# A forward and backward of a recurrent-memory transformer block on one core: merged dP products, a planner with later landings, and Wo turned in runs

## The chip, the cores and the metric

The kernel runs on one core of a Trainium2 chip. The metric is the time of one execution in microseconds on the device, the median of several runs; lower is better.

## The reference

For x of 2048 tokens by 512, xn = layernorm(x), and the output is x + A(xn) + B(xn).

B is a dense layer pair: h = relu(xn w1 + b1) squared, then h w2 + b2, with w1 of 512 by 1792.

A is an attention with a recurrent memory. The 2048 tokens are cut into 64 segments of 32. For each segment in order, the 8 memory rows are put ahead of its 32 tokens, and 32 heads of width 128 attend over these 40 rows:

```
h = concatenate([mem, xs]);  q, k, v = h Wq, h Wk, h Wv
p = softmax(where(mask, q k^T * scale, -1e9));  o = p v;  o = o Wo
mem = o[:, :M];  outs.append(o[:, M:])
```

The mask lets the memory rows see everything and the tokens see what lies before them. Segment s+1 needs the memory of segment s, so the 64 segments are a chain. The task also asks for the gradients of all ten differentiable inputs for a given grad_out, so the same chain is walked a second time, from the last segment to the first.

## The kernel before, in words

The kernel works in stages, one after the other, all on one core.

The dense part computes the layernorm, B forward and most of B's backward in eight blocks of 256 tokens. It loads w1, w2 and b1 first (L887 to L895), turns w2 and w1 by TensorE transposes (turn_w, L838), and stores the hidden activations and their gradients to DRAM (S_AT, S_GT1).

The forward recurrence walks 64 steps, 16 blocks of four. A step (chain, L1136) projects q, k and v of its 32 rows for all heads (Stage.proj, L530, 32 products of 512 columns each), copies them out of PSUM, transposes q and k, forms scores, takes the softmax weights into the tile P40, multiplies with v, transposes the result, multiplies with Wo (wo_part, L1030) and brings the 8 new memory rows to the next step. q, k, v, P and o are written to DRAM for the backward. Four heads' products stand side by side in four groups of 32 columns of the array, so that four products run together. What is not on this path is filled in around it: the "leading" tokens (the eight rows of each segment that stand in the memory's places, 32 per block: l_proj, l_attn), the outputs of a block (blk_out, L1214) and the weight gradients of w1 and w2 (dw_unit, L1238: for two column blocks at a time, 16 products each with a 128-row block of tokens that is loaded from DRAM into one of five tiles sx).

At the end of this stage, turn_o (L497) turns Wo in place: eight transposes go into one PSUM bank, and two copies bring them back to SBUF. The heads' inner index is taken up in four strides of the bank, so that each copy reads PSUM with jumps.

The backward recurrence walks the steps from the last to the first. A step (chain, L1454) multiplies the step's gradient rows with the turned Wo (gO), copies it to gN, transposes it (gOT), forms dP with the stored v (L1468, products of 40 columns), goes through the softmax backward on VectorE (smax_bwd, L1350, four operations), forms dv, dk and dq (blocks, mixed, diag), transposes each (sq_T, L513) and multiplies with the turned Wv, Wk, Wq into one PSUM bank (dh_part, L1363, ps_dRA); the 8 rows of that sum are the memory gradient that the next step needs (L1524). A block's leading tokens are handled by l_pre (L1381) and l_post (L1420); l_pre forms their dP (ps_dPL, L1404), once against the leading v (VTL) and once against the memory-place v (VTM, the tile LT1), each with products of 32 columns. l_post reads back their gradients from DRAM into dLN and adds ps_dRL.

The last stage computes the gradients of Wq, Wk, Wv and Wo from what was stored (L1690, L1694) and, beside it, the layernorm backward.

The order of the instructions in the first three stages is drawn up when the kernel is built, by a planner (the class _Plan). Every operation has an engine, a cost in microseconds, keys that it reads and writes, and for DMAs a latency after which its data are taken to have landed. The planner ranks the operations by the longest way to the end plus a bias from a table (BIAS_1, BIAS_2; one number for each operation of a scope), then fills the engines' queues in simulated time. PAR gives three parameters for each stage: a grace for operations of low priority, how long an engine is held idle for something better, and a penalty for changing the shape of TensorE's products. The planner also models how TensorE's instructions arrive: in lines of 128 products, a line no sooner than 4.2 us after the one before. That count starts with each stage. The order within each engine's queue is then fixed, and an engine waits at the head of its queue until the data are there. SyncE (SP) issues most DMAs, GpSimd (POOL) some.

The helpers Stage.put and Stage.dma (L474, L477) give a DMA its cost (0.5 on POOL, T_DMA = 0.42 on SP) and latency (3.5 and 3.2 unless given); dmaT (L1376) gives a transposing load 1.35 and 3.2. evict (L526) is a copy out of PSUM for which the planner chooses VectorE or ScalarE.

Of the kernel before, what the change touches and what calls it, by code (L numbers as in the profile page):

```python
# [12 lines left out]
BIAS_1 = {  # L13
    "l_proj": (
        47.2, 6.5, -41.1, 1.2, 0.8, -33.9, -14.2, 11.4, 20.3, -5.1, -5.3, -14.4, 17.4, 1.5, 7, 20.1, 4.7,
        25.3, -22.2, 55.6, -37, 19.3, -97.5, -1.4, 23, -6.1, -29.3, 48.8, 4.1, 4.5, 52.1, -159.3,
    ),
    "blk_in": (
        11.4, -35.6,
    ),  # L20
# [4 lines left out]
    ),  # L25
    "chain": (
# [4 lines left out]
    ),  # L31
    "blk_out": (
        16.8, -102.8, -36.2, -171.6, -10.2, -72.7, -50.6, -74.7, -96.5, 48.6,
    ),
    "l_attn": (
# [45 lines left out]
P = 128  # L81
# [227 lines left out]
def kernel(  # L309
# [148 lines left out]
    class Stage:  # L458


        def __init__(self, plan, pool, ways):
            self.plan = plan
            self.pool = pool
            self.ways = ways
            self.cnt = {}
# [1277 lines left out]
```

## Time and profile before

| | |
|---|---|
| time, median of 3 runs | 2799.88 us (2797.52 to 2802.31) |
| span of the profiled execution | 2798.3 us |
| TensorE: products, weight loads | 54888 recorded, 55072 |
| TensorE busy | 2664.6 us (95%) |
| VectorE, ScalarE, GpSimd busy | 1327.3, 985.8, 824.8 us |
| DMA | 530.91 MB, 190 GB/s |
| granted TensorE clock | 0.995 |

The span runs from the first to the last instruction of one execution that was profiled; its own time is this span and the little that lies around it, and the median of the timed runs is 1.6 us above the span. In the rows of the profile PE is TensorE's products, PEld its weight loads, DVE is VectorE, ACT ScalarE, POOL GpSimd and SP the engine that issues DMAs; a q behind an engine's name is its sequencer. A group row has the line, the engine, the operation, what it writes and reads, shapes and count, then busy microseconds and the mean in nanoseconds of one, then the idle time before it with what ended that. A row of waits has the waiting instruction, what it waited for, the total in microseconds, how often, and the longest. A row of the timeline has start and length in microseconds. Some records of products are missing in a trace, so weight loads are the better count.

### The profile page before, as it was taken

Reading aid. Unit: us, or ns where it says so; the run is one execution under the profiler, and the core shown is the slowest. Engines: PE = TensorE matmul, PEld = TensorE weight load, DVE = VectorE, ACT = ScalarE, POOL = GpSimd, SP = SyncE. Lnnn points to the kernel's source line nnn. Section 1 sums busy time; section 2 is a strip of 40 time slices with the busy share of each in tenths; the row PEclk is TensorE's granted clock in tenths of the full one; section 3 lists DMA queues with packets and bytes.
Section 4 is the critical chain, followed back from the end, with each engine's and each line's share of the span. In section 5 each row is a group of like instructions: output and inputs, shape, how many; then the busy total and the mean of one; then the engine's idle time right before and its main releaser. Section 6 shows DMA issues by size and latency. Waiting matters only on the chain.

```text
span 2798.3 us, 125071 instructions
## 1 busy us (share of the span) xinstructions
PE 2664.6 (95%) x54888; PEld 1538.5 (55%) x55072; DVE 1327.3 (47%) x3327; ACT 985.8 (35%) x2012; POOL 824.8 (29%) x2431
## 2 busy tenths in 40 slices
PE   8998999999999999999999999999999899999999
PEld 6664555555555555575555555555555444444444
DVE  5544455555455555565455455555455402232322
ACT  4333444444444444364444444444444300000000
POOL 1111111111111111145555555555555301112210
PEclk9999999999999999999999999999999999999999
DMA  6657656555557566647777676777766698788861
GB/s 211 202 172 205 180 160 175 164 166 163 156 169 186 169 185 175 177 118 178 187 181 187 179 189 179 189 192 190 188 182 177 201 344 273 232 255 270 257 185 42
DMA packets 499792, 530.91 MB, mean 190 GB/s; under 512 B 223845, under 2 KB 325398, under 8 KB 497070
## 3 DMA queue, kind: packets, MB, share of 16 engines
q1 hardware_dynamic: 480254, 463.06, 59.9%
q0 software_dynamic: 15056, 53.56, 5.6%
q8 instruction: 430, 7.05, 1.1%
q10 hardware_dynamic: 3936, 6.29, 0.7%
q14 instruction: 116, 0.95, 0.1%
HBM read 249.77 MB, written 237.52 MB: 174 GB/s over the span
## 4 chain that ended last, share of the span: by engine, by line
PE 45%; DVE 4%; issue 3%; DMA 3%; ACT 1%; POOL 1%; SPq 0%; DVEq 0%; ACTq 0%; POOLq 0%
PE ps_gw L1690 14%; PE ps_dRA L1370 8%; PE ps_gw L1694 5%; PE ps_gO L538 3%; PE ps_dRL L1370 3%; PE ps_d L624 2%; DMA dLN<-S_GNL 2%; PE ps_d L573 1%; PE ps_d L599 1%; PE ps_gOT L429 1%; PE ps_d L588 1%; PE ps_gm L1524 1%; PE ps_gL L538 1%; PE ps_dL L1481 1%; PE ps_dP L1468 1%
## 5 line engine op out<-in xcount | busy, mean ns | idle before, releaser
L1370 PE MATMUL ps_dRA<-WA,dT 128*32 128x512 bf16 x6144 | 377.0, 381 | 5.3 <-issue 2.5
L1690 PE MATMUL ps_gw<-WA,WB 128*128 128x512 bf16 x1505 | 330.6, 379 | 1.6
L1690 PEld LDWEIGHTS <-WB 128*128 128x128 bf16 x1896 | 185.4, 98 | 225.0 <-issue 1.7
L538 PEld LDWEIGHTS <-PA 128*32 128x32 bf16 x8192 | 195.4, 96 | 192.3 <-DVE PA L1190 22.3
L435 ACT CAST dN<-ps_d 128x512 bf16<-128x512 f32 x372 | 207.4, 590 | 184.7 <-PE ps_d L599 112.3
L1370 PEld LDWEIGHTS <-dT 128*32 128x32 bf16 x6144 | 151.8, 96 | 154.2 <-DVE dT L517 17.3
L433 DVE CAST gwo<-ps_gw 128x512 bf16<-128x512 f32 x64 | 40.0, 685 | 399.9 <-PE ps_gw L1690 268.5
L435 ACT CAST gwo<-ps_gw 128x512 bf16<-128x512 f32 x64 | 33.1, 598 | 510.2 <-PE ps_gw L1690 357.3
L517 DVE STREAM_TRANSPOSE dT<-dN 128x256 f32<-128x256 f32 x384 | 165.4, 437 | 72.1 <-ACT dN L435 66.5
L1020 POOL TENSOR_TENSOR P<-P,rsA 128x320 bf16<-128x320 bf16 x64 | 46.2, 722 | 458.8 <-DVE rsA L1015 244.1
L624 PEld LDWEIGHTS <-PB 32*32 32x32 bf16 x8192 | 119.8, 92 | 76.4 <-DVE PB L1168 23.9
L1701 POOL DMA_DIRECT2D out_dram<-gwo x96 | 71.6, 753 | 293.9 <-ACT gwo L435 265.1
L538 PE MATMUL ps_q<-WA,PA 128*32 128x512 bf16 x2048 | 145.2, 382 | 5.5 <-DVE PA L1190 3.7
L1039 PE MATMUL ps_RA<-WB,OT 128*32 128x256 bf16 x4096 | 129.0, 277 | 17.7 <-DVE OT L517 13.6
L538 PE MATMUL ps_k<-WA,PA 128*32 128x512 bf16 x2048 | 144.9, 381 | 0.3 <-DVE PA L1190 0.3
L435 ACT CAST kN<-ps_k 128x512 bf16<-128x512 f32 x125 | 73.4, 587 | 194.1 <-PE ps_k L538 172.2
L538 PE MATMUL ps_v<-WA,PA 128*32 128x512 bf16 x2048 | 140.7, 379 | 0.0
L1039 PEld LDWEIGHTS <-OT 128*32 128x32 bf16 x4096 | 103.9, 98 | 46.2 <-DVE OT L517 32.0
L538 PE MATMUL ps_gO<-WB,PA 128*32 128x512 bf16 x2048 | 126.4, 380 | 1.0 <-DVE PA L1528 1.0
L611 POOL COPY BDL<-bPLL 32x64 bf16<-32x64 bf16 x256 | 60.4, 236 | 218.4 <-PE ps_d L573 210.4
L433 DVE CAST qN<-ps_q 128x512 bf16<-128x512 f32 x62 | 42.9, 692 | 171.5 <-PE ps_q L538 169.5
L1254 PE MATMUL ps_dw<-sx,anT 128*128 128x512 bf16 x339 | 108.2, 384 | 6.6 <-DMA sx<-S_XN 2.8
(315 smaller groups left out, 5300.8 us busy)
## 6 DMA issues: line engine op xcount, KB each, us to landing
S_GN<-dN SPq DMA_DIRECT2D x192, 256.0 KB
WA<-S_GN SPq DMA_DIRECT2D x150, 256.0 KB
S_Q<-qN SPq DMA_DIRECT2D x64, 256.0 KB
S_K<-kN SPq DMA_DIRECT2D x64, 256.0 KB
S_V<-vN SPq DMA_DIRECT2D x64, 256.0 KB
S_ON<-oN SPq DMA_DIRECT2D x64, 256.0 KB
bqN<-S_Q SPq DMA_DIRECT2D x64, 256.0 KB
bkN<-S_K SPq DMA_DIRECT2D x64, 256.0 KB
```

What stands on the lines that cost most here:

```text
L433: nc.vector.tensor_copy(out, in_)
L435: nc.scalar.copy(out, in_)
L517: self.plan.add({"DVE": 0.445}, lambda e, half=half: nc.vector.transpose(words(dst, half).rearrange("p (i c r) -> p i c r", i=4, c=2), src ...
L538: nc.tensor.matmul(bk()[32 * j:32 * (j + 1), :], lhsT=win(dc), rhs=Wt(dc, c0), start=(dc == 0), stop=(dc == DC - 1), tile_position=(0, 32 ...
L611: f(q_(dst, j)[:, :, j, 0:c], q_(src_f(), j))
L624: nc.tensor.matmul(bk()[32 * j:32 * j + m, k * P:(k + 1) * P], lhsT=lf(j, i), rhs=rf(j, i), start=(k == 0 and x == 0), stop=(x == n - 1), ...
L1039: nc.tensor.matmul(bk()[32 * c:32 * (c + 1), :], lhsT=sg.rows(OTt, i, j), rhs=Wo[:, JQ * i + j, dh * DH:(dh + 1) * DH], start=(i == 0 and ...
L1254: nc.tensor.matmul(bks[x]()[:], lhsT=anT[x][:, c, :], rhs=sx[z][:], start=(c == 0), stop=(c == TC - 1))
L1370: nc.tensor.matmul(bk()[32 * j:32 * (j + 1), :], lhsT=sg.rows(XT, i, j), rhs=wtf(t, i, j), start=(first and i == 0), stop=(last and i == N ...
L1690: nc.tensor.matmul(bks[n](), lhsT=HNc[:, rc, dc * P:(dc + 1) * P], rhs=gns[y][:, hf * 512:(hf + 1) * 512], start=(y == 0), stop=(y == NRC ...
L1694: nc.tensor.matmul(bks[n](), lhsT=gns[y][:, k * P:(k + 1) * P], rhs=GOc[:, rc, :], start=(y == 0), stop=(y == NRC - 1))
L1701: nc.gpsimd.dma_start(outWs[t][dc * P:(dc + 1) * P, 4 * hf:4 * hf + 4, j, :], wt[:].rearrange("p (i e) -> p i e", i=4))
```

## The change

The change consists of these parts.

- The load of b1 (dense part): 14 rows of 128 numbers, then a TensorE transpose into a PSUM bank and a copy, in place of a load that scatters b1 down the partitions. The loads of w1, w2 and the first gradient block get a planned latency of 2.6 and a cost of 0.85.
- Forward: two tiles P40 that alternate by step; hN is put into the tile PTLL; the token blocks of dw_unit are loaded two at a time into three tiles; the copies into S_VM, S_KM, S_BL, S_HNL and S_GOL are costed at 0.7; the tiles mk and mkl of the masks move into the dense part's pool.
- Planner: PAR and BIAS_1, BIAS_2 are new in all numbers of the two recurrences. Both recurrences are planned with slow = True: DMAs cost 0.47 (SP) and 0.62 (POOL), and latencies below 4.5 are raised by 1.0. In the backward a transposing load costs 1.45 with a latency of 4.2.
- Turn of Wo: the copies read PSUM and write SBUF in runs of 32 numbers. The heads' inner index is thus left in another order, and the copies of gO and gL out of PSUM put it right, reading in steps of 32.
- Five products of the identity with itself are put behind the forward's plan.
- Backward, l_pre: VTL and LT1 become thirds of one tile V3, so that one product of 64 columns takes both. 32 products in place of 64 for each block.

The helper mixed gets three more arguments that no call uses.

```diff
-PAR = ((0.3, 0.3, 0.0), (0.61, 7.94, 4.04), (0.09, 2.05, 17.32))
+PAR = ((0.3, 0.3, 0.0), (0.38, 999.0, 10.03), (0.09, 1.77, 17.22))
...
-        def put(self, out_f, in_f, R, W, prio=1, lat=3.5, cost=0.5):
+        def put(self, out_f, in_f, R, W, prio=1, lat=3.5, cost=None):
+            cost = cost or (0.62 if self.slow else 0.5)
             self.dma(out_f, in_f, R, W, prio, lat, cost, "POOL")
-        def dma(self, out_f, in_f, R, W, prio=1, lat=3.2, cost=T_DMA, eng="SP"):
+        def dma(self, out_f, in_f, R, W, prio=1, lat=3.2, cost=None, eng="SP"):
+            cost = cost or (0.47 if self.slow else T_DMA)
+            if self.slow and lat < 4.5:
+                lat += 1.0
...
-                    self.evict(lambda blk=blk, d=d0 + d: blk[:, :, d * P:(d + 1) * P].rearrange("p j (a c) -> p j a c", c=JQ), bk,
-                               lambda bk=bk, d=d: bk()[:, d].rearrange("p c (j a) -> p j a c", j=JQ), [(okey, g, d)], 1, {"DVE": 0.61, "ACT": 0.59})
+                    self.evict(lambda blk=blk, d=d0 + d: blk[:, :, d * P:(d + 1) * P].rearrange("p j (c a) -> p j c a", c=JQ), bk,
+                               lambda bk=bk, d=d: bk()[:, d].rearrange("p c (j a) -> p j c a", j=JQ), [(okey, g, d)], 1, {"DVE": 0.37, "ACT": 0.59})
...
+                if nm in ("gO", "gL"):
+                    self.evict(lambda half=half: dst[1][:, 4 * half:4 * half + 4, :].rearrange("p i (a c) -> p i a c", c=JQ),
+                               bk, lambda bk=bk: bk()[:].rearrange("p (i c a) -> p i a c", i=4, c=JQ), [(dst[0], half)], prio, EV_F)
+                    continue
...
-                        sg.dma(lambda: b1Tb[:], lambda: B_b1.rearrange("(c p) -> p c", p=P), [], ["b1Tb"], lat=5.0)
+                        sg.dma(lambda: b1Tb[:], lambda: B_b1.rearrange("(c p) -> c p", p=P), [], ["b1Tb"], lat=5.0)
...
-                A({"DVE": 0.1}, lambda e: V.tensor_copy(b1T[:], b1Tb[:]), ["b1Tb"], ["b1T"])
+                bb1 = sg.bank("B", [P, FC], BF16, "ps_b1")
+                A({"PE": 0.1}, lambda e: transpose_to(bb1()[:], b1Tb[:]), ["b1Tb"], [bb1])
+                A({"DVE": 0.1}, lambda e: V.tensor_copy(b1T[:], bb1()[:]), [bb1], ["b1T"])
...
-                z = c % 5
-                sg.dma(lambda z=z: sx[z][:], lambda c=c: src[c * P:(c + 1) * P, :], [], [("sx", z)], lat=3.0)
+                z = c // 2 % 3
+                if c % 2 == 0:
+                    sg.dma(lambda z=z: sx[z][:], lambda c=c: src[c * P:(c + 2) * P, :].rearrange("(c p) d -> p c d", p=P), [], [("sx", z)], lat=3.2)
...
+        with tc.manual_schedule():
+            al = pc.tile([P, 512], F32, name="ps_al", tag="c0")
+            for x in range(5):
+                nc.tensor.matmul(al[:, 0:P], lhsT=ident[:], rhs=ident[:], start=True, stop=True)
...
-        LT0, LT1 = (tl("LT%d" % x, TR) for x in range(2))
+        LT0, V3 = tl("LT0", TR), tl("V3", [P, 3, NI, JQ, RA])
+        VTL, LT1 = [V3[:, 1], V3[:, 0]], V3[:, 2]
+        V2 = [V3[:, 1:3], V3[:, 0:3:2]]
...
-            A({"SP": 1.35}, lambda e: nc.sync.dma_start_transpose(out_f(), in_f()), R, W, prio, 3.2)
+            A({"SP": 1.45}, lambda e: nc.sync.dma_start_transpose(out_f(), in_f()), R, W, prio, 4.2)
...
                 for i in range(NI):
-                    for c, VX in enumerate((VTL[p], VTM)):
-                        for j in range(JQ):
-                            nc.tensor.matmul(q_(bk(), j)[:, i, 32 * c:32 * c + 32], lhsT=LT0[:, i, j, :],
-                                             rhs=VX[:, i, j, :], start=(i == 0 and c == 0), stop=True,
-                                             tile_position=(0, 32 * j), skip_group_check=True)
-            A(pe(0.45, "w", 64), dp, both("LT0") + both("LT1") + [("VTL", p)], [bk, "btL"])
+                    for j in range(JQ):
+                        nc.tensor.matmul(q_(bk(), j)[:, i, :], lhsT=LT0[:, i, j, :], rhs=V2[p][:, :, i, j, :],
+                                         start=(i == 0), stop=True, tile_position=(0, 32 * j), skip_group_check=True)
+            A(pe(0.3, "w", 32), dp, both("LT0") + both("LT1") + [("VTL", p)], [bk, "btL"])
```

More of the change, by code (lines that the diff above doesn't have):

```diff
@@ L458, with __init__ @@
     class Stage:
-        def __init__(self, plan, pool, ways):
+        def __init__(self, plan, pool, ways, slow=False):
             self.plan = plan
+            self.slow = slow
             self.pool = pool
@@ L694 @@
     maskL = fww.tile([P, NI, 2 * RL], BF16, name="maskL")
-    for i in range(NI):
-        nc.vector.tensor_copy(maskA[:, i, M:KA], mk[:])
     with tc.tile_pool(name="p0", bufs=1) as p0, \
             tc.tile_pool(name="pp", bufs=1, space=bass.MemoryType.PSUM) as pp:
+        mk = p0.tile([P, RA], BF16, name="mk")
+        nc.gpsimd.memset(mk[:], 0.0)
+        for j in range(JQ):
+            nc.gpsimd.affine_select(
+                q_(mk, j), q_(mk, j), pattern=[[-1, RA]], compare_op=ALU.is_ge, fill=NEG, base=0, channel_multiplier=1
+            )
@@ L699 @@
+        for i in range(NI):
+            nc.vector.tensor_copy(maskA[:, i, M:KA], mk[:])
         RB = 2 * P
@@ L970 @@
         qT, OT = (tl(n, TR) for n in ("qT", "OT"))
-        P40 = tl("P40", [P, NI, KA])
+        P40s = [tl("P40%d" % x, [P, NI, KA]) for x in range(2)]
         PTA, PTL = (pb_rest[:, x * HW // 4:(x + 1) * HW // 4].rearrange("p (i k) -> p i k", i=NI) for x in range(2))
@@ L978 @@
         m2 = tl("m2", [P, DH], F32)
-        hN = tl("hN", [P, D])
         sm_t = {}
```

167 lines of the change are left out of this document (90 added, 77 removed), and 48 rows, old and new, of tables (BIAS_1, BIAS_2).

## The prediction

> **What bounds the kernel now.** I read the page first (busy time and the chain), then a table of five stretches, then, for each edit, the groups, the timeline or the waits of the place where it acts.
>
> ```profile
> span 2798.3 us, 125071 instructions
> PE 2664.6 (95%) x54888; PEld 1538.5 (55%) x55072; DVE 1327.3 (47%) x3327; ACT 985.8 (35%) x2012; POOL 824.8 (29%) x2431
> ...
> q8 instruction: 430, 7.05, 1.1%
> ...
> PE 45%; DVE 4%; issue 3%; DMA 3%; ACT 1%; POOL 1%; SPq 0%; DVEq 0%; ACTq 0%; POOLq 0%
> ```
>
> TensorE (PE) is busy 95% of the span; VectorE, next, 47%. (The q8 row has packets, megabytes and a share.) The chain could be followed back only over its later part, and there PE holds 45 of the some 57 points that it names. The stretches are: the dense part (to 227 us), the forward recurrence (to 1209), the turn of Wo between the stages (to 1236), the backward recurrence (to 2245), the weight gradients (to the end). The columns are length, then busy time and instructions of each engine.
>
> ```profile
> 0.00:227.00 227.00, 213.93 (x1519) 145.13 (x1543) 118.05 (x481) 85.90 (x208) 36.36 (x84) 1.00 0.60 190
> 227.00:1209.00 982.00, 919.39 (x23629) 550.12 (x23735) 520.51 (x1278) 433.13 (x893) 142.84 (x264) 0.99 0.62 173
> 1209.00:1236.00 27.00, 22.27 (x364) 21.37 (x360) 22.02 (x39) 17.65 (x27) 12.11 (x31) 0.94 0.60 142
> 1236.00:2245.00 1009.00, 962.31 (x26896) 573.25 (x26893) 520.00 (x1290) 415.44 (x820) 539.64 (x1916) 1.00 0.71 184
> 2245.00:2798.30 553.30, 546.75 (x2506) 248.64 (x2545) 146.73 (x240) 33.73 (x65) 93.84 (x137) 1.00 0.74 231
> ```
>
> PE stands idle 13 us in the dense part, 63 in the forward, 5 in the turn, 47 in the backward, 7 at the end: 134 us are all that any reordering can win by closing idle time, and in the two recurrences a busy PE is not yet one that issues at its best rate. The two recurrences, 1991 us, are the ones whose order of instructions a planner writes, and the change gives that planner new tables and new costs. So this is a PE-bound kernel in which most of the effect hangs on the order.
>
> **The change part by part.** *The load of b1.* Before, its 1792 numbers are scattered down the partitions, each a piece of its own. The timeline of the first 16 us:
>
> ```profile
> 1.24 1.49 SPq L479 DMA_DIRECT2D W<-in_B_w_dram  x3
> ...
> 7.72 0.60 SPq L479 DMA_DIRECT2D xN<-in_A_x_dram  x1
> ...
> 8.37 0.60 SPq L479 DMA_DIRECT2D b1Tb<-in_B_b_dram  x1
> ...
> 9.01 6.45 SPq L479 DMA_DIRECT2D WB<-in_B_w_dram  x5
> ...
> 13.48 0.63 ACT L759 ACTIVATE maskL<-xN 128x512 bf16<-128x512 bf16 x1 [5.44 <-DMA xN<-in_A_x_dram]
> ...
> 15.14 1.01 PE L429 MATMUL ps_W2T<-ident,W 128*128 128x128 bf16 x8 [3.08 <-DVE WB L433]
> ```
>
> Ahead of b1 three weight issues take 1.49 us, 0.50 each. Behind it five take 6.45, 1.29 each: 4 us more than at the first pace. The x rows issued just ahead of b1 keep ScalarE waiting 5.44 us, and ScalarE and VectorE then free PE late: 3.08 us idle. After, b1 comes as 14 rows, one transpose of 14 columns is added on PE (one product; 8 of them take 1.01 us here, so about 0.13) and the vector copy stays. I take 2.5 us of the 3.08 as won; the bounds are 0 (the weights alone fill the queue) and 4.0 (all of the slow issues). The new costs of these loads in the dense part's planner can move their order, which I count in these bounds.
>
> *The forward plan.* Two-block loads in the products for w1 and w2 (112 issues fewer), a second tile for P, hN kept in PTLL, the copies of S_V and S_K costed at 0.7, latencies raised by 1.0, three new parameters, five new tables. The masks' move to another pool changes no instruction. The second P tile adds none; it removes a wait on the S_P write. What hN now waits for (the readers of PTLL) is off the step's own path and comes once in four steps; PE's other work covers it, and if it did not, each of 16 blocks would lose up to a landing (5.61 us, row below), 90 us at the very worst. What the order can win is seen by rates: 23735 weight loads in 982 us are 24.2 per us. The best 200 us of the forward and of the backward:
>
> ```profile
> 500.00:700.00 200.00, 188.98 (x4976) 114.08 (x4992) 108.50 (x265) 90.53 (x190) 27.13 (x51) 1.00 0.57 165
> ```
> ```profile
> 1700.00:1900.00 200.00, 195.54 (x5504) 115.80 (x5500) 105.49 (x263) 83.41 (x166) 111.44 (x397) 1.00 0.74 191
> ```
>
> 4992 in 200 us are 25.0 per us; at that rate the whole forward takes 951 us, 31 less. A new plan may as well lose as much. I take a quarter as won, 8 us, with 31 lost and 31 won as ends.
>
> *The turn of Wo.* Groups of the stretch 1205 to 1225, then like copies with straight runs from the list of groups, then the timeline at its end:
>
> ```profile
> L433 DVE COPY WB<-ps_Wo 128x512 bf16<-128x512 bf16 x15 | 9.2, 685 | 3.5 <-ACT WB L435 3.4
> L435 ACT COPY WB<-ps_Wo 128x512 bf16<-128x512 bf16 x17 | 8.8, 604 | 3.3 <-DVE WB L433 3.1 <-PE ps_Wo L429 0.2
> ```
> ```profile
> L435 ACT CAST gON<-ps_gO 128x512 bf16<-128x512 f32 x127 | 74.4, 586 | 98.1 <-PE ps_gO L538 98.1
> ...
> L433 DVE COPY KT<-ps_kT 128x512 bf16<-128x512 bf16 x124 | 47.3, 420 | 0.4 <-PE ps_kT L429 0.4
> ...
> L435 ACT COPY qT<-ps_qT 128x512 bf16<-128x512 bf16 x61 | 35.8, 586 | 19.4 <-PE ps_qT L429 18.9 <-PE ps_kT L429 0.6
> ```
> ```profile
> 1221.74 2.44 PE L429 MATMUL ps_Wq<-ident,WA 128*128 128x128 bf16 x24 [4.08 <-ACT WB L435]
> ```
>
> 32 copies read PSUM with jumps: 685 ns on VectorE, 604 on ScalarE. Both together clear 1/0.685 + 1/0.604 = 3.12 per us, 10.3 us in all, and PE waits 4.08 us for the last before the backward's first product. In runs of 32 VectorE should need 420 (the KT row, which also writes in runs); 1/0.420 + 1/0.604 = 4.04 per us, 7.9 us. I take the difference, 2.4 us, as won; it can't exceed 4.08. The five extra products on the identity stand ahead of the backward: 1.01 us for 8 is 0.13 each, 0.6 us at most, behind the same copies. Their use can only be a shift of the backward's place in the instruction stream (below).
>
> The jumps do not vanish: the copies of gO and gL now read PSUM in steps of 32 numbers, 128 for gO and 32 for gL. For two-byte data the jump costs ScalarE 604 against 586, 3%. For four-byte data no row shows it. From below: nothing. From above: as much more as the jump costs VectorE, 685/420 = 1.63 times, 0.37 us on each copy. By the nearest row, 604 against 586, and since these copies run on ScalarE, I take nothing. PE's wait for it:
>
> ```profile
> PEld L429 <- ACT gON L435: 20.8, 48, 0.7
> ```
>
> *The leading tokens' dP.* One block's products in the timeline: 64 of 32 columns (first, last, and what follows), and two neighbours with 40 and 128 columns:
>
> ```profile
> 1241.20 0.38 PE L1468 MATMUL ps_dP<-bVT,gOT 128*32 128x40 bf16 x32
> 1241.42 0.25 PE L1481 MATMUL ps_dL<-gON,BPK 128*32 128x128 bf16 x4
> 1241.48 0.25 PE L1481 MATMUL ps_dL<-gLN,BLK 128*32 128x128 bf16 x4
> ...
> 1243.44 0.20 PE L1404 MATMUL ps_dPL<-VTL,LT 128*32 128x32 bf16 x4
> ...
> 1243.90 0.21 PE L1404 MATMUL ps_dPL<-LT,LT 128*32 128x32 bf16 x4
> 1243.93 0.84 PE L1370 MATMUL ps_dRA<-WA,dT 128*32 128x512 bf16 x12
> ```
>
> From 1243.44 to 1243.93 are 0.49 us for 16 groups of four. Four of 40 columns take 0.22/8 = 0.0275 us, four of 128 take 0.06. Eight groups of 64 columns then lie between 0.22 and 0.48; on the line between the two, 0.035 each, 0.28 in all. That saves 0.21 us a block, 3.4 us in 16 blocks (bounds 0.2 and 4.3). PE is bound here, so I count it whole.
>
> *The backward plan.* Landings planned 1.0 later, transposing loads 1.45, queue costs 0.47 and 0.62, new parameters and six new tables. What the old plan got wrong, from the waits between 1262 and 2215 and the chain:
>
> ```profile
> DVE LT L517 <- DMA dLN<-S_GNL: 36.9, 22, 2.9
> ...
> PE ps_dP L1468 <- issue: 6.2, 9, 0.9
> ...
> PE ps_dL L1481 <- issue: 5.3, 4, 2.5
> ```
> ```profile
> 1823.19 5.61 DMA dLN<-S_GNL
> ```
>
> VectorE stands 22 times at the head of its queue for dLN, 36.9 us, with the step's own operations queued behind it: the plan reckoned 4.0 for a landing that took 5.61. The new one reckons 5.0. PE also waits 11.5 us on two lines for nothing that the profile names, which I read as its instructions arriving: 109,960 recorded PE instructions came in 430 blocks, 256 each. Sixteen times 32 products fewer, with their weight loads 1024 instructions, are 4 blocks fewer. Rates again: 26893 in 1009 us are 26.7 per us, the best window has 27.5 and would make it 978, 31 less. Because two wrong costs are mended here, I take a third as won, 10 us; ends 31 either way.
>
> The Trainium skill's "Runtime: NRT & Kernel Launch", section "Instruction fetch mechanics", says that instructions are refilled in 16 KiB blocks and that crossing a block is mostly hidden. By that rule the five products and the place of a block's edge change nothing. The trace agrees on the block (7.05 MB in 430) and, with the unnamed waits above, leans against "hidden".
>
> The weight gradients are not touched: nothing there.
>
> **Sum.** 2.5 + 8 + 2.4 + 3.4 + 10 = 26.3, less 0.6 for the five products and 0.1 for b1's: 25.6 us won. The profiled span is 2798.3; 1.6 us lie between it and the median, 2799.9. So 2799.9 - 25.6 = 2774.
>
> **The rivals.** *Only the local edits pay.* The new order is as good as the old one; 2.5 + 2.4 + 3.4 - 0.7 = 7.6 us stay: 2792. For it: busy PE in the forward is already 94%, and the waits for dLN are VectorE's, while PE found other work in most of them. Against it: the new costs lie nearer to what the trace shows. *The change does not do what it says:* the later landings move no instruction that PE waits for, and a block's edge is hidden or lies as badly as before; the time is the same 2792, so I put both into one case.
>
> *The new order is slower.* The step's own work (gO, dP, the four softmax operations, dS, dRA) is queued behind work put ahead of it on VectorE and PE in expectation of late data. Place: 126 steps of the two recurrences. Price: 0.3 us a step is 38 us, with the local 7.6 that is 2830; at 0.06 us a step (7.6/126) the local gains are eaten up. For it: a step is 1009/64 = 15.8 us, so 0.3 is 2%, and tables drawn up for one set of costs fit the chip only as far as the costs do.
>
> *The stepped PSUM read costs the chain.* 64 steps wait for the first gO copy; at the upper end, 0.37 us each, 24 us are lost, and the rest wins 25.6: 2798. For it: PE waits for this copy in 48 places already (20.8 us). Against it: the 604 against 586 on ScalarE.
>
> **How the numbers follow.** Forecast, at 2774 with 2750 to 2792 of its own: 0.60. Local edits only, 2792 (2786 to 2800): 0.19. Slower order, 2830 (2806 to 2845): 0.14. Stepped read, 2798 (2792 to 2804): 0.07. The bound of what can be told from no change is 0.2%, 5.6 us: 2794.3 and 2805.5. Faster takes 0.59 of the first, 0.11 of the second and 0.01 of the last; slower 0.14 of the third and 0.01 of the last; the rest, 0.14, is the same. The range 2745 to 2812 leaves out about one chance in ten above and a little less below.
>
> **What would show it.** b1: the five weight issues behind it near 0.5 us each and PE's 3 us wait gone. Wo: VectorE's 15 copies near 420 ns and the 4.08 us wait shorter by some 2. gO: ScalarE's copies still near 586. dP: 32 products in 0.28 us. Plan: the backward's wait of VectorE for dLN below 20 us, its length near 995, the forward's near 974, more than 27 and 24.4 weight loads per us. The prediction is wrong if either recurrence gets longer, above all if PE waits more for VectorE's maskA, dT or gON copies.

## The result

The changed kernel takes 2791.89 us, the median of 9 runs (2782.14 to 2797.71), against 2800.61 us for the kernel before in the same series (9 runs, 2797.52 to 2810.6). The ratio is 0.9954, with a 95% interval of 0.9942 to 0.9967: 13 us faster, between 9 and 16 (the two medians lie 8.7 apart, the spans of the two profiled executions 6.5). The forecast was 25.6 us. All ratios below are to the kernel before, run beside the kernel in question on the same chip; a difference between two such ratios carries both intervals, some 6 us either way.

First the head of the page of the changed kernel, then the same five stretches as in the prediction (length, then busy time and instructions of PE, PEld, DVE, ACT and POOL).

```profile
span 2791.8 us, 124115 instructions
PE 2665.3 (95%) x54566; PEld 1526.3 (55%) x54566; DVE 1366.4 (49%) x3397; ACT 952.6 (34%) x1969; POOL 826.0 (30%) x2431
...
q8 instruction: 426, 6.98, 1.1%
```
```profile
0.00:227.00 227.00, 217.89 (x1595) 145.69 (x1599) 120.49 (x496) 86.25 (x209) 36.19 (x84) 1.00 0.63 195
227.00:1209.00 982.00, 929.22 (x23839) 556.54 (x23828) 538.14 (x1307) 433.47 (x914) 149.39 (x274) 0.99 0.61 173
1209.00:1236.00 27.00, 26.96 (x544) 22.81 (x542) 22.99 (x43) 19.38 (x24) 13.78 (x45) 1.00 0.80 143
1236.00:2245.00 1009.00, 947.97 (x26086) 555.19 (x26085) 538.09 (x1312) 380.33 (x758) 533.70 (x1893) 0.99 0.75 186
2245.00:2791.80 546.80, 543.30 (x2517) 246.09 (x2515) 146.70 (x240) 33.13 (x64) 92.97 (x136) 1.00 0.75 228
```

The cuts are those of the kernel before, so the changed kernel is further along at each of them. In the first three stretches PE is busier than before (217.9 for 213.9, 929.2 for 919.4, 27.0 for 22.3). In the fourth it is less busy: 948.0 for 962.3, so that PE stands idle 61 us where it stood 47.

Where the steps lie is read from the first and last start of two small products that each step has once: ps_mem in the forward, ps_gm in the backward (63 steps each, so 62 step lengths between). For the kernel before:

```profile
L1185 PE MATMUL ps_mem<-sel,PB x504: 169/172/196, 249.3 to 1188.7; 128*32 128x16 bf16 x168
L1524 PE MATMUL ps_gm<-sel,R_A x2016: 169/176/198, 1259.2 to 2209.1; 128*32 128x8 f32 x184
```

and for the changed kernel:

```profile
L1207 PE MATMUL ps_mem<-sel,PB x504: 169/172/185, 249.9 to 1180.2; 128*32 128x16 bf16 x168
L1551 PE MATMUL ps_gm<-sel,R_A x2016: 172/176/198, 1243.1 to 2202.0; 128*32 128x8 f32 x184
```

The forward's 62 steps went from 939.4 to 930.3 us. The backward begins 16.1 us earlier, and its 62 steps went from 949.9 to 958.9: 9.0 us longer, where the forecast had 13.4 less (10 for the plan, 3.4 for dP). So the sign came that the prediction had named for being wrong, a recurrence that gets longer. In this pair of executions more than half of what had been won is given back there. The rest of this document asks why.

The local edits show in the trace as follows; first the start of the dense part.

```profile
5.33 2.09 SPq L483 DMA_DIRECT2D W<-in_B_w_dram  x2
...
7.46 1.99 SPq L483 DMA_DIRECT2D WB<-in_B_w_dram  x2
...
11.07 2.92 SPq L483 DMA_DIRECT2D WB<-in_B_w_dram  x3
```

With b1 as rows the weight issues still take 1.0 us each, not 0.5. Next come the groups of copies in the turn of Wo with that of gO, then PE's timeline at the turn's end, then dP's place in a block:

```profile
L432 DVE COPY WB<-ps_Wo 128x512 bf16<-128x512 bf16 x20 | 6.9, 413 | 2.1 <-PE ps_Wo L428 2.1
L434 ACT COPY WB<-ps_Wo 128x512 bf16<-128x512 bf16 x12 | 6.3, 592 | 1.5 <-DVE WB L432 1.4
```
```profile
L434 ACT CAST gON<-ps_gO 128x512 bf16<-128x512 f32 x128 | 74.9, 585 | 118.5 <-PE ps_gO L542 117.4 <-PE ps_gOT L428 0.6 <-DMA bkLN<-S_KL 0.5
```
```profile
1207.27 0.44 PE L1321 MATMUL ps_al<-ident 128*128 128x128 bf16 x5
1208.25 1.95 PE L428 MATMUL ps_Wk<-ident,WA 128*128 128x128 bf16 x32 [0.54 <-ACT WB L434]
```
```profile
1226.31 0.42 PE L1432 MATMUL ps_dPL<-V,LT 128*32 128x64 bf16 x32
1226.55 0.45 PE L1495 MATMUL ps_dP<-bVT,gOT 128*32 128x40 bf16 x32
```

VectorE's copies fell from 685 to 413 ns, the wait for the last copy from 4.08 to 0.54 us. ScalarE's stepped copies of gO stay at 585. From dP's first product to the next group are 0.24 us, where there were 0.49. Last, the waits in the backward (window 1262 to 2215):

```profile
PEld L1399 <- issue: 18.7, 42, 2.1
PEld L644 <- issue: 18.4, 30, 1.7
...
DVE LT L521 <- DMA dLN<-S_GNL: 20.3, 10, 3.9
```

VectorE's wait for dLN was 36.9 us and is 20.3. But PE's weight loads now stand 37.1 us on two lines for "issue", for nothing that the profile names. In the kernel before, the largest such row for a weight load in this window is this one:

```profile
PEld L429 <- issue: 9.0, 22, 0.5
```

The waits for VectorE and ScalarE that the prediction had named as the danger did not grow, taken together (weight loads for maskA 12.9 us after 15.1, for dT 11.3 after 17.3, for gON 23.3 after 20.8). New are two waits of PE's products for loads, 8.1 us between 1236 and 2245; the kernel before has no row of PE for a DMA there:

```profile
PE ps_d L618 <- DMA bqN<-S_Q: 5.7, 3, 2.2
...
PE ps_dqL L644 <- DMA V<-S_KM: 2.4, 4, 1.0
```

### The profile page after: what moved, and what is told of

It is laid out like the page before. It is cut to its first block, busy times and chain, and to the rows that moved or that the text cites. A ratio compares the mean times of both kernels' runs of the same rounds, so it can differ in the third digit from the quotient of the medians.

```text
span 2791.8 us, 124115 instructions
## 1 busy us (share of the span) xinstructions
PE 2665.3 (95%) x54566; PEld 1526.3 (55%) x54566; DVE 1366.4 (49%) x3397; ACT 952.6 (34%) x1969; POOL 826.0 (30%) x2431
## 5 line engine op out<-in xcount | busy, mean ns | idle before, releaser
L434 ACT CAST dN<-ps_d 128x512 bf16<-128x512 f32 x336 | 189.5, 589 | 168.4 <-PE ps_d L618 93.0
L1216 POOL TENSOR_TENSOR obA<-obA,PB 64x256 bf16<-64x256 bf16 x64 | 42.5, 663 | 508.2 <-DVE PB L1068 403.2
L1060 PE MATMUL ps_RA<-WB,OT 128*32 128x256 bf16 x4096 | 130.1, 277 | 10.4 <-DVE OT L521 9.7
L1278 PE MATMUL ps_dw<-sx,anT 128*128 128x512 bf16 x448 | 118.1, 381 | 1.9 <-issue 1.3
L434 ACT CAST gON<-ps_gO 128x512 bf16<-128x512 f32 x128 | 74.9, 585 | 118.5 <-PE ps_gO L542 117.4
L1399 PE MATMUL ps_dRL<-WA,LT 128*32 128x512 bf16 x1536 | 109.5, 384 | 3.7 <-DVE LT L521 2.6
```

The lines of the kernel that those rows point to most:

```text
L434: nc.scalar.copy(out, in_)
L1060: nc.tensor.matmul(bk()[32 * c:32 * (c + 1), :], lhsT=sg.rows(OTt, i, j), rhs=Wo[:, JQ * i + j, dh * DH:(dh + 1) * DH], start=(i == 0 and ...
L1216: A({"POOL": 0.665}, lambda e: nc.gpsimd.tensor_tensor(out=hf(obA, p)[:, v, :], in0=hf(obA, p)[:, v, :], in1=hf(mb, p), op=ALU.add), [("mb ...
L1278: nc.tensor.matmul(bks[x]()[:], lhsT=anT[x][:, c, :], rhs=sx[z][:, c % 2, :], start=(c == 0), stop=(c == TC - 1))
L1399: nc.tensor.matmul(bk()[32 * j:32 * (j + 1), :], lhsT=sg.rows(XT, i, j), rhs=wtf(t, i, j), start=(first and i == 0), stop=(last and i == N ...
```

## What the unnamed stalls are

The two rows above are read from the trace's records of PE's instructions and of the packets of queue q8. If PE's instructions are counted through (two for a product, one for a semaphore event), the gaps without a cause bunch at one place in 256, at each edge of a block, and each block is one packet (430 edges and 430 packets before, 426 and 426 after). One such edge in the changed kernel's timeline:

```profile
1413.01 1.03 PE L1399 MATMUL ps_dRA<-WA,dT 128*32 128x512 bf16 x13
1414.91 0.83 PE L1399 MATMUL ps_dRA<-WA,dT 128*32 128x512 bf16 x12 [0.88 <-issue]
```

A row of 25 products is torn after 13. PE passed the edge before at 1409.80. The packet began at 1411.55, 1.75 us later, took 2.12 us, was over at 1413.67, and PE went on 1.25 us after that. The other edges show the same order of events. In the kernel before, PE never goes on less than 1.20 us after its packet's end (198 edges between 1265 and 2195 us; in the changed kernel one of 192 edges is at 1.14; the median over the edges with a stall above 0.5 us is 1.38), and 95% of the packets begin more than 0.19 us after the edge before. So one block is fetched ahead, no more. From an edge until the next block is usable are 3.83 us in the median (delay 1.42, packet 1.13, landing 1.25), and 4.35 or more in a quarter of the cases. PE's own work in a block, by which I mean the time between two edges less the stall (waits for other engines are in it), has a median of 4.57 us and is below 4.25 in a quarter. Where the work is shorter than the fetch, PE's weight loads stand for about the difference: that difference, taken edge by edge from the packets, correlates with the stalls seen at 0.97 in the kernel before and 0.98 in the changed one. The forward's blocks hold 5.2 us of work, and the stalls at its edges are 9.8 us in all before and 15.5 after.

Here is the count for all kernels below. Steps are the 62 step lengths of forward and backward; stalls is the sum of unnamed gaps above 0.15 us in the row of the weight loads (PEld) at the edges of the backward's blocks, 1265 to 2195 us. One profiled execution each: kernels with the same order differ by up to 15 us in the forward column (934.9 to 949.8) and by up to 10 in the backward one (948.7 to 958.9), and a profiled execution need not lie at its kernel's median (that of dP in 32 columns, 2816.5 us, is the longest of its 12).

```
kernel (order of fwd/bwd)           forward backward stalls   ratio [95%]
before (old/old)                      939.4    949.9   25.0   1
b1 as rows (old/old)                  949.3    950.2   27.0   1.0001 [0.9985, 1.0016]
Wo in runs (old/old)                  937.9    954.3   27.1   1.0002 [0.9988, 1.0016]
dP 64 columns (old/old)               934.9    940.4   22.5   0.9981 [0.9966, 0.9996]
all three local (old/old)             949.8    947.6   27.7   0.9968 [0.9951, 0.9985]
dP 64 + wide gm (old/old)             940.3    955.2   13.7   1.0005 [0.9990, 1.0021]
new forward alone, dP 32 (new/old)    925.0    966.8   38.9   1.0001 [0.9988, 1.0013]
the same, dP 64 (new/old)             928.6    964.6   38.8   0.9965 [0.9948, 0.9982]
changed kernel (new/new)              930.3    958.9   35.1   0.9954 [0.9942, 0.9967]
  without the five products           926.2    952.2   30.6   0.9932 [0.9912, 0.9953]
  22 of them                          929.9    954.9   32.1   0.9954 [0.9934, 0.9974]
  54                                  935.7    948.7   35.4   0.9945 [0.9926, 0.9965]
  86                                  928.8    955.5   43.8   0.9972 [0.9955, 0.9990]
  dP in 32 columns                    930.7    975.0   46.7   1.0006 [0.9989, 1.0023]
  32 one-column products a block      928.2    965.0   47.6   1.0001 [0.9984, 1.0018]
  96 one-column products a block      927.9   1010.0   53.0   1.0169 [1.0133, 1.0204]
  wide gm                             924.3    961.8   22.9   0.9977 [0.9961, 0.9993]
old tables, dP planned new (new/-)    926.6   1124.3    5.2   1.0529 [1.0512, 1.0547]
```

Two things bound what the table can carry. First, a gap of the weight loads is not a gap of the products: at the edge shown the loads stand 1.36 us and the products 0.88, because a product still at work covers a part. The products' own waits for "issue" between 1236 and 2245 us add up to 17.8 us in the kernel before, 20.3 in the changed one and 28.3 with the new forward alone. Second, the clock: the traces list stretches in which the granted clock is halved. Between 249 and 1175 us they are 10 to 31 us (mean 21.1) in the six kernels with the old forward order and 0 to 12 (mean 4.8) in the twelve with the new one; in the 62 backward steps they are 3.4 us before and 17.1 in the changed kernel. A halved clock can cost at most half of its stretch, so up to 8 us of the forward's gain and up to 7 of the 9.0 us above may be the clock. Whether the orders and stalls bring these stretches about is not shown.

## The experiments

**Where the backward begins in its block.** The first theory was that the five products put the edges at bad places, the rival that the place matters little.

```diff
-            for x in range(5):
+            for x in range(22):
```

> The changed kernel with 22 products of the identity in place of 5: the order of all other work is the same, and only the place of the edges of the 256-instruction blocks moves, by 17 products, to where the planner's own count of lines puts the first edge. Theory 1 (blocks: the new backward loses at the edges of instruction blocks, where TensorE stood 43.6 us unnamed in the changed kernel's backward and 26.8 before): the edges' share moves by 10 us or more, here downwards, and the time goes to 2776 to 2786. Theory 2 (order: the new order is longer wherever the edges lie): the time stays at 2792 plus 1 us for the products, 2791 to 2795.

> The changed kernel with 54 products of the identity: the edges move by 49 products against the change, everything else is in the same order. Theory 1: another share at the edges, the time differs from 2792 plus 2.7 us for the products by 5 us or more either way, and the trace's stall at the edges differs by as much. Theory 2: 2793 to 2797.

> The changed kernel with 86 products of the identity: the edges move by 81 products. Theory 1: the time differs from 2792 plus 4.5 us by 5 us or more either way, in step with the stall at the edges. Theory 2: 2794 to 2799.

> The changed kernel without the five products of the identity, so that the backward starts 10 instructions earlier in its block. If their place matters little, as with 17, 49 and 81 more: within 4 us of the changed kernel, 2788 to 2796. If the five put the edges of blocks where the plan reckons with them: 2797 or more.

Measured: 2789.04, 2786.46 and 2794.32 us, and 2788.45 without any. (The 43.6 and 26.8 us in these expectations come from an earlier count of the stalls; the table has 35.1 and 25.0.) The ratios go from 0.9932 to 0.9972, in nearly the order of the stalls (30.6 to 43.8). All intervals but those of the extremes overlap, and these just miss each other, 11 us apart. So the place of the edges counts for some us, but no place tried brings the forecast, which is a ratio of 0.991. The five products do not help: the kernel without them is the fastest measured. Its lead over the changed kernel (0.9932 against 0.9954, intervals overlapping) is not established; both beat the kernel before.

**The old backward tables under the new list.** The changed kernel with the old tables, parameters, costs and latencies in the backward, dP planned at its new cost.

```diff
-PAR = ((0.3, 0.3, 0.0), (0.38, 999.0, 10.03), (0.09, 1.77, 17.22))
+PAR = ((0.3, 0.3, 0.0), (0.38, 999.0, 10.03), (0.09, 2.05, 17.32))
...
-            A({"SP": 1.45}, lambda e: nc.sync.dma_start_transpose(out_f(), in_f()), R, W, prio, 4.2)
+            A({"SP": 1.35}, lambda e: nc.sync.dma_start_transpose(out_f(), in_f()), R, W, prio, 3.2)
```

> The changed kernel with the backward planned as before: its table, its three parameters, costs and latencies of DMAs as before; all else (64-column dP, runs in Wo's turn, the forward) as changed. If the new plan of the backward is what lost (both theories), its backward of 958 us for 62 steps falls to 940 to 950 and the time to 2773 to 2784. Theory 1: the stall at the edges falls from 43.6 us to below 35. Theory 2: the edges stay near 43.6 and the gain is in waits for VectorE and ScalarE. If the backward's loss came with the 64-column products or the stepped reads of gO instead, the time stays at 2788 to 2796.

Measured: 2950.89 us. A single planned cost (dP 0.3 for 0.45) makes the planner draw up another order with the old tables, and it is 160 us worse. The wait rows of its backward (1262 to 2350) show the step's own chain queued behind other work:

```profile
POOL BPK L633 <- PE ps_dL L1510: 390.5, 55, 12.7
...
PEld L620 <- DVE maskA L1390: 108.4, 52, 6.6
```

In the changed kernel the second of these rows is:

```profile
PEld L618 <- DVE maskA L1388: 12.9, 24, 1.6
```

So this run says nothing of the new tables; it shows that a table is good for its own list and costs only. It also bears on the mechanism: the blocks there last 5.7 us in the mean without the stalls, and the edges' stalls are 5.2 us in all.

**The old backward order in the changed kernel.** With dP planned at 0.45 the old order comes back, operation by operation on every engine. It ran with dP emitted in 64 and in 32 columns.

```diff
-            A(pe(0.3, "w", 32), dp, both("LT0") + both("LT1") + [("VTL", p)], [bk, "btL"])
+            A(pe(0.45, "w", 64), dp, both("LT0") + both("LT1") + [("VTL", p)], [bk, "btL"])
```

> The changed kernel, but the backward is planned with the kernel before's tables, parameters, costs and latencies, and dP with its old planned cost of 0.45, while 64-column products are emitted. So the backward's order is that of the kernel before, operation by operation; all else is as changed. Theory A (the new backward plan is itself worse by some 8 us than the old one, and the other edits pay): 62 backward steps in 944 to 949 us, VectorE waits for dLN near 49 us again, time 2778 to 2786, faster than the changed kernel. Theory B (the two plans are worth the same, and the longer backward of the changed kernel's profile is chance or the place of block edges): 62 steps in 952 to 960 us, time 2788 to 2795.

> The changed kernel with the whole backward of before: its order, its planned costs, and dP in 64 products of 32 columns. So the dense part, the forward and the turn alone are new. If these are what the change gains: forward's 62 steps near 930 us against 939, dense part and turn some 6 us shorter, backward near 950, time 2786 to 2792, as fast as the changed kernel. If the forward's gain is chance: 2797 to 2803.

Measured: 2794.95 and 2801.28 us. In the first the 62 steps take 964.6 us, more than either theory had. The second is the run that decides. Dense part, forward and turn are new, and the backward starts 20 us earlier; the total is that of the kernel before. Its rows:

```profile
L1209 PE MATMUL ps_mem<-sel,PB x504: 169/172/184, 249.7 to 1174.7; 128*32 128x16 bf16 x168
L1555 PE MATMUL ps_gm<-sel,R_A x2016: 169/176/222, 1238.6 to 2205.4; 128*32 128x8 f32 x184
```

The same instructions in the same order take 966.8 us where the kernel before takes 949.9; 10 to 14 of these 17 us are stalls at the edges (28.3 against 17.8 by the products' own waits, 38.9 against 25.0 by the weight loads). It is not the local edits, which leave the backward as it was in the old order (947.6 and 27.7 with all three). The place in the block is the same to one instruction, so the two runs can be compared edge by edge. The fetch of a block takes 3.98 us in the mean against 3.91, and it is the fetches that make the difference: fetch less work, added up over the edges where the fetch is the longer, is 20 us in the kernel before and 28 here; with the fetches of this run and the work of the kernel before it is 31, the other way round 19. The packets come later at the short blocks; what delays them behind the new forward is not settled.

**The local edits one by one.**

```diff
 (b1 as rows; kernel before)
-                        sg.dma(lambda: b1Tb[:], lambda: B_b1.rearrange("(c p) -> p c", p=P), [], ["b1Tb"], lat=5.0)
+                        sg.dma(lambda: b1Tb[:], lambda: B_b1.rearrange("(c p) -> c p", p=P), [], ["b1Tb"], lat=5.0)
...
 (dP in 32 columns; changed kernel)
-                        nc.tensor.matmul(q_(bk(), j)[:, i, :], lhsT=LT0[:, i, j, :], rhs=V2[p][:, :, i, j, :],
+                            nc.tensor.matmul(q_(bk(), j)[:, i, 32 * c:32 * c + 32], lhsT=LT0[:, i, j, :],
+                                             rhs=V2[p][:, c, i, j, :], start=(i == 0 and c == 0), stop=True,
```

The others carry the change's own lines for Wo, gO and dP into the kernel before, with its planned costs.

> The kernel before with b1 loaded as 14 rows and turned by TensorE, nothing else. If b1's scattered load caused the dense part's gain: first q product of the forward 3 to 4 us earlier (near 225), time 2796 to 2798. If the new costs and latencies of the weight loads caused it: first q product near 228.5 and no difference to the kernel before.

> The kernel before with Wo turned in runs and gO and gL copied out with steps of 32, at the old planned costs, so that the order stays; nothing else. If runs pay and the stepped four-byte read costs nothing: VectorE's copies of WB near 415 ns, 2 to 4 us less between the last forward step and the first backward step, time 2796 to 2798. If the stepped read costs the chain: ScalarE's gO copies above 650 ns and the time above the kernel before's.

> The kernel before with the leading tokens' dP as 32 products of 64 columns a block, in the kernel before's order throughout; nothing else. Theory A (a product less is worth its work and its share of the instructions' arrival, in any order): 4 to 14 us faster than the kernel before, 2789 to 2799. Theory B (a fixed order is fitted to where its blocks of instructions end; fewer instructions move those places, and the gain goes into stalls at them): within 3 us of the kernel before or slower, 2800 to 2808, with the unnamed stalls at every 256th TensorE instruction of the backward above the 29 us or so that they take in the old list.

> The kernel before, in its order, with the three local edits together: b1 in rows, the turn of Wo in runs with the stepped copies of gO and gL, dP in 64 columns. By the forecast's local terms 7.6 to 8.3 us faster than the kernel before, 2793 to 2795. If each is worth what it was alone (nothing, nothing, 5.3): 2796 to 2798. If the local edits are also what lengthens the backward behind the new forward: 2800 or more.

> The changed kernel in the order that it has, with the leading tokens' dP emitted as 64 products of 32 columns a block in place of 32 of 64. It undoes one local edit. If TensorE's time counts whole here (16 blocks, 0.49 against 0.24 us, and 4 instruction blocks more): 3 to 6 us slower than the changed kernel, 2795 to 2798. If the 0.25 us a block are covered by other waits, or the edges of the blocks shift to better places: 2790 to 2793, no difference.

Measured: b1 2804.35 and runs 2800.76 us, both no difference; dP alone 2796.32, 0.9981, that is 5 us (1 to 10); the three together 2797.34, 0.9968, that is 9 us (4 to 14). Undoing dP in the changed kernel costs 0.0052 of 2800, 14.6 us, more than any theory gave it. Two rows of the timeline for b1 (SP's queue, then PE) and one for Wo:

```profile
9.51 4.60 SPq L479 DMA_DIRECT2D WB<-in_B_w_dram  x5
```
```profile
15.90 1.01 PE L429 MATMUL ps_W2T<-ident,W 128*128 128x128 bf16 x8 [3.33 <-DVE WB L433]
```
```profile
1220.45 1.76 PE L429 MATMUL ps_Wq<-ident,WA 128*128 128x128 bf16 x15 [3.13 <-ACT WB L435]
```

With b1 as rows five weight issues still take 0.92 each (1.29 before), and PE's 3 us wait stays: the weights alone keep the queue slow enough. With Wo in runs the 4.08 us wait falls to 3.13 only; the changed kernel's 0.54 comes of the new planned cost, which gives 20 of the 32 copies to VectorE in place of 15.

**Work or instructions?** dP's 512 products more cost 14.6 us, their work 16 times 0.25, 4.0. So the count itself was put to the test: products of one column with zeros, and in the other direction fewer, wider products.

```diff
+                for x in range(1):
+                    for i in range(NI):
+                        for j in range(JQ):
+                            nc.tensor.matmul(q_(bk(), j)[:, i, 0:1], lhsT=LT0[:, i, j, :], rhs=zcol[:], start=False,
+                                             stop=True, tile_position=(0, 32 * j), skip_group_check=True)
...
-                            for j in range(JQ):
-                                nc.tensor.matmul(q_(bm(), j)[:, dc, :], lhsT=R_A[:, dc * P + 32 * j:dc * P + 32 * (j + 1)],
-                                                 rhs=sel8[:], start=(dc == 0), stop=True, tile_position=(0, 32 * j),
+                            nc.tensor.matmul(bm()[:, dc, :], lhsT=R_A[:, dc * P:(dc + 1) * P], rhs=sel8[:],
+                                             start=(dc == 0), stop=True, skip_group_check=True)
```

> The changed kernel, and behind each block's dP 32 products of one column with a column of zeros, added to the same sums (the result is unchanged): as many TensorE instructions as in the run with 64 products of 32 columns, with less work. Theory A (instructions arrive no faster than a block of 256 in some 4.2 us, and the backward runs close to that): 8 to 14 us slower than the changed kernel, 2800 to 2806. Theory B (they cost TensorE's own time alone, at most the 0.24 us of 32 products of 64 columns, 3.8 us in 16 blocks): 2792 to 2796.

> As the run before, with 96 products of one column behind each block's dP, 12 blocks of 256 instructions more in all. Theory A: 25 to 45 us slower than the changed kernel, 2817 to 2837. Theory B: 96 at no more than 7.5 ns, 0.72 us in each of 16 blocks, up to 11.5 us slower, 2796 to 2804.

> The changed kernel, in its order and with its planned costs, but the eight memory-gradient rows of a step (ps_gm) are formed by 4 products with 128 columns of weights in place of 16 with 32 in four groups: 8 recorded products for 32 a step, 1512 fewer in 63 steps, 11.8 blocks of 256 instructions. Theory A (arrival of instructions counts; 512 products more cost 13 us when they were added): 25 to 40 us faster than the changed kernel, 2752 to 2767. Theory B (TensorE's own work counts): the 32 take 0.77 us in the trace of the changed kernel; 8 with wider weights between 0.3 and 0.9 us, so from 30 us faster to 8 slower; told apart from A by the stalls at the blocks' edges, which stay as they are under B and shrink with the number of blocks under A.

> The kernel before, in its order, with dP in 64 columns and the memory-gradient rows in 4 wide products. If the gain of fewer products does not hang on the plan: as much faster than the run with dP alone as the changed kernel gains by the same edit, 25 to 40 us, 2756 to 2771. If a plan gains only from what it was drawn up for: less than 10 us.

Measured: 2800.40 and 2848.51 us for one-column products, 2798.68 and 2809.36 for wide gm. First the timeline with 32 one-column products, then with dP in 32 columns:

```profile
1222.49 0.42 PE L1434 MATMUL ps_dPL<-V,LT 128*32 128x64 bf16 x32
1222.73 0.43 PE L1439 MATMUL ps_dPL<-zcol,LT 128*32 128x1 bf16 x32
1223.01 0.46 PE L1502 MATMUL ps_dP<-bVT,gOT 128*32 128x40 bf16 x32
```
```profile
1230.41 0.66 PE L1433 MATMUL ps_dPL<-V,LT 128*32 128x32 bf16 x64
1230.90 0.46 PE L1497 MATMUL ps_dP<-bVT,gOT 128*32 128x40 bf16 x32
```

32 products of one column hold PE 0.28 us, no less than 32 of 64 columns (0.24). In 16 blocks that is 4.5 us; the edges' stalls rise by 12.5 (47.6 for 35.1); together 17, measured 13.2 (0.0047 of 2800), though the steps of the profiled execution are only 6.1 longer (965.0 against 958.9). dP in 32 columns: 4.0 of work and 11.6 of stalls, 15.6, measured 14.6. With 96 one-column products the sum does not close: 0.81 us a block (1222.67 to 1223.48 in its timeline), 13 us, and 17.9 of stalls make 31, measured 60; VectorE waits 41.7 us for these sums (10.4 in the changed kernel), and in the 62 backward steps the clock is halved for 54.6 us (17.1 in the changed kernel), which can be up to 19 of the missing 29. All six runs of this kernel have a lower granted clock (0.983 to 0.989) than the nine of the changed kernel (0.992 to 0.996). Why the clock is lower there is open.

The wide memory-gradient products, the changed kernel's rows first:

```profile
1706.78 0.77 PE L1551 MATMUL ps_gm<-sel,R_A 128*32 128x8 f32 x32
```
```profile
1701.23 1.06 PE L1550 MATMUL ps_gm<-sel,R_A 128*128 128x8 f32 x8
```
```profile
L1551 PEld LDWEIGHTS ps_gm<-sel,R_A x1920: 106/112/113, 1272.7 to 2187.7; 128*32 128x32 f32 x192
```
```profile
L1550 PEld LDWEIGHTS ps_gm<-sel,R_A x488: 186/192/193, 1266.7 to 2198.5; 128*128 128x128 f32 x163
```

8 wide ones last 1.06 us, 32 narrow ones 0.77: a step has 0.29 us more work, 18.0 in 62 steps, and on its own chain. The stalls fall by 12.2 us (22.9 for 35.1). The sum is 5.8 slower, measured 6.4 (0.9977 against 0.9954). In the old order the same sum is 18.0 less 8.8, 9.2, measured 6.7. Both measured differences are only just clear of their intervals. So neither theory held alone: PE's work and the stalls of arrival both count. Fewer instructions did not bring the gain that Theory A had, and work alone leaves out the stalls. That the two simply add up is supported by the ratios, within some 6 us and except for the 96 products; the steps of single executions differ from these sums by up to 11 us without them.

## Why the prediction was wrong, step by step

- **The load of b1, 2.5:** the stage gained, the reason was wrong. The first q product of the forward moved from 228.5 to 224.7 us, but b1 in rows alone moves nothing; the lower bound that I had named (the weights alone fill the queue) came true. The 3.8 us come from the new costs and latencies of these loads or their order, which were not tried apart.
- **The forward plan, 8:** right in its direction, and too small. Over the kernels run, the old order's 62 steps take 941.9 us in the mean (6 kernels), the new one's 928.5 (12): 13.4, of which up to 8 may be the clock. The quarter of a rate that I took was a guess, and which of the forward's edits won was not tried apart; that the sign is right says little for the reasoning.
- **The turn of Wo, 2.4:** the size of the copies was right (413 ns for 420 forecast), and the wait shrank by 3.5. By the layout alone it shrank by 1.0; the planned cost did the rest.
- **The stepped gO copies, nothing:** right, 585 ns for 586. That rival is out.
- **The five products, 0.6:** 0.44, and no use found for them.
- **dP in 64 columns, 3.4:** the work was right (0.24 us a block, forecast 0.28), the price mis-sized: 5 us in the old order, 14.6 in the changed one. I counted "4 blocks fewer" and gave them no price.
- **The backward plan, 10:** this is the step that failed. VectorE's wait for dLN did fall to 20.3 us, nearly as forecast, but it was hardly a wait of PE: the time that I counted on PE for it did not come, and PE's products now wait 8.1 us for loads, where they waited for none. With the same dP, the new backward order against the old one is worth 0.9954 against 0.9965, 3 us at 64 columns, and 1.0006 against 1.0001, nothing, at 32; both within their intervals. This holds behind the new forward; the new backward order was not run behind the old one.
- **The sum:** I added up stages as if each kept its gain. Of the 20 us by which the new first stages bring the backward forward, 17 are lost again in an unchanged backward, 10 to 14 of them at the edges of the instruction blocks. The rates that I took as a goal (the best 200 us of each stage) leave that limit out.

The rival *only the local edits pay* named the time that came, 2792, and the three local edits in the old order do give 9 us for the 7.6 forecast. But as a mechanism it is half right: the new forward order is not without effect, it wins in its own stage, and the backward behind it loses that again, in the old order as in the new. Of the rule of the Trainium skill ("Runtime: NRT & Kernel Launch", "Instruction fetch mechanics") the first half holds: blocks of 256, the next one fetched while the present one runs. That the crossing is mostly hidden holds for the forward's blocks of 5.2 us (9.8 us of stalls in the kernel before); in the backward, at 4.57 us against a fetch of 3.83 in the median, the weight loads stand 25 us in the kernel before and 47 in the changed kernel with dP in 32 columns.

What stays open: why the packets come later in an unchanged backward behind the new forward, which part of the new forward does it, and how much of the differences is the granted clock. The runs exclude the local edits and the starting place in the block.

## What to carry to other kernels

Where small products follow each other closely, look at queue q8 beside PE: count 256 instructions a block, compare PE's own work in a block with the fetch of the next, and price an edit by work plus the change of these stalls, not by the length of its products. Read the stalls in the products' row as well as in the weight loads', and the granted clock beside them. A gain in one stage is not a gain of the kernel until the next stage has been timed behind it: the run that had only the new first half told more than all local rows. And an order table belongs to one list of operations and costs; try an edit alone with the planned costs left as they were, in the old order and in the new.

## What the runs showed of the hardware that was not expected

- One block of 256 TensorE instructions is fetched ahead: in the kernel before, 95% of the backward's packets start more than 0.19 us after the edge before (median 1.42 us), and PE goes on no sooner than 1.20 us after the packet's end (1.01 at one edge of the run with 96 products).
- A product of one column costs PE as much as one of 64 columns when four stand side by side: 32 take 0.28 and 0.24 us.
- Four-byte weights of 128 columns load in 192 ns, of 32 columns in 112, so 8 wide products (1.06 us) lose to 32 narrow ones (0.77).
- A stepped read of PSUM in two-byte numbers cost VectorE 685 ns for 413 in runs; in four-byte numbers it cost ScalarE nothing (585 for 586).
